# Decay products and one key-value product over 128 tokens in a fused recurrence and two-layer network kernel, with a third PSUM bank for the first matmul of a step

## The chip, the cores and the metric

The kernel runs on one core of a Trainium2 chip. The metric is device time in microseconds (us) of one execution, as the median of several. The engines go by their names in the profile: PE (matmul), PEld (its weight load), DVE (vector), ACT (activation), POOL (GpSimd) and SP, which here only issues DMAs.

## The reference

Inputs are double precision for the weights and single precision for the rest. Three parts follow one another:

```
state = 0                                   # per batch (4) and head (8), 48 x 48
for t in range(768):
    y[t]  = r[t] @ (state + (u * k[t]) (x) v[t])
    state = w[t][:, None] * state + k[t] (x) v[t]
x = y as 3072 x 384
h = x @ w_in;  g = h if h >= 1, 0 if h <= -1, else (h + 1)^2 / 4;  x = g @ w_out     # 384 -> 2048 -> 384
h = x @ w2_in; g = h * sigmoid(1.702 h);                            out = g @ w2_out
```

w lies between 0.8 and 0.95, so the product of the decays over 128 tokens gets very small (0.8 to the power 128 is 4e-13).

## The kernel before, in words

**The recurrence** (`window(n)`, lines 406 to 538) is done in 24 windows of 128 tokens (6 per batch), each for all 8 heads. A window has two chunks of 64 tokens, c = 0 and c = 1. Heads are paired: `hh` says which half of the partitions a head has, `m` which of the four pairs. The decays are multiplied up inside each chunk: a scan from the right (line 423) gives `rr`, the product of the decays to the end of the chunk, its reciprocal seeds a scan from the left (425) that gives `pp`. k is multiplied by `rr` (430, DVE, in place) and r by `pp`: in place for windows 0 to 6 (433, one 128x512 on POOL), into the tiles `ra` for the later ones (437, two 64x512 on POOL). `pcs` is a copy of the eight chunk products (429, DVE). PE then transposes k (464, tile `tp`, copied to `ktok` by ACT, 471) and forms the scores (469, tile `sc`); DVE's masked copy puts the scores into the other half of `ra` (474), over a diagonal that POOL writes there (455). For windows 0 to 6 ACT copies the scaled r into `ra` after the scores (484). PE multiplies keys by values for both chunks (498, one PSUM tile per chunk, rows 64c to 64c+63 of the array, the four pairings of row half and column half in the order of `ORDER`), and y for chunk 0 (504). The operand `lt` of the y product holds, per chunk, the state (48 partitions of one half) and the values (64 partitions of the other half). The state goes on by `upd(c)` (510, DVE: `lt` of chunk c plus the key-value product into the tile `us`) and `put(us, c)` (446, POOL: `us` times `pcs` into `lt` of a chunk): `put(carry, 0)` at the start of a window, `put(upd(0), 1)` in the middle. ACT sums squares of the decays (449, 450) and of r and k (486) for a check of the number range.

**The two layers** go by `step(s)` (260): a step is one tile of 384 tokens and one of 16 slices of 128 hidden columns; 8 tiles make 128 steps per layer. Step s issues, in this order: `gemm1` into the PSUM tile `hp` (651, nine matmuls of 384 columns: each operand is split in a high and a low part), DVE's clamp (688) and ACT's square (689) of it, the low part of g of the step before (676, on POOL and DVE by turns), then one turn of the recurrence, `gemm2` of step s-3 into the three accumulators (660, nine matmuls; 669 in the second layer), DVE's maximum with `hp` (701), which is the last reader of `hp`, ACT's high part of g (682), weight work and, in every second step, one more turn of the recurrence. `hp` comes from a pool of two PSUM banks by turns, so `gemm1` of a step waits for line 701 of two steps before. In a turn every running window goes on to its next `yield`; a new window starts when the one before has had eight turns (four at the very start). The recurrence for tile i+1 runs beside the first layer of tile i.

**The weights** come as double precision and are put together as single precision: DVE 638, ACT 640, DVE 642, POOL 644 (`wide`). The first layer's 32 pieces are done in the opening, the second layer's (`conv_w2`, 194) one in every second step of tiles 1 to 6: the four operations, ACT's check of the piece (147, 148), the load of a new piece and the store to `w2_d` (196) are issued in the same step.

**PSUM** has eight banks: three accumulators, two for `hp`, three (`ps_s`) for `tp`, `sc`, `yt`, `kv0` and `kv1`. When the recurrence is over, `hp` has four.

**Order.** Up to step 15 a planner orders the instructions of each engine by modelled times and priorities (the opening). From step 16 on (`manual_schedule`) each engine does its instructions in the order of the program.

Of the kernel before, what the change touches and what calls it, by code (L numbers as in the profile page):

```python
# [9 lines left out]
F32 = mybir.dt.float32  # L10
# [3 lines left out]
AF = mybir.ActivationFunctionType  # L14
# [16 lines left out]
WW = MC * (C + 1)  # L31
# [3 lines left out]
ORDER = ((0, 0), (0, 1), (1, 1), (1, 0))  # L35
PMIN = 1e-10
# [14 lines left out]
K_E = (1,)  # L51
PI_B = 1
RIP_N = 7
# [48 lines left out]
def fast_path(st, tc, rkw_t, nat, v_l, w1, w2, u, out, x2_d, w2_d, flag_i, force):  # L102
# [4 lines left out]
    ps_h = st.enter_context(tc.tile_pool(name="ps_h", bufs=2, space=PSUM))  # L107

# [41 lines left out]
    def to_f32(l, n):  # L150
# [9 lines left out]
        wide(nc, [x[1:] for x in todo])  # L160
# [4 lines left out]
        return [(x[0], x[3].bitcast(F32)) for x in todo]  # L165
# [27 lines left out]

    def conv_w2():
        for i, wf in to_f32(1, PRE_N):
            nc.sync.dma_start(out=w2_d[:, i, :], in_=wf)

# [24 lines left out]
    pools = {"h": [ps_h], "x2": None}  # L222
# [37 lines left out]
    def step(s):  # L260
# [79 lines left out]
    with ExitStack() as sa:  # L340
        at = sa.enter_context(tc.tile_pool(name="at", bufs=1))
        a2 = sa.enter_context(tc.tile_pool(name="a2", bufs=2))
        ps_s = sa.enter_context(tc.tile_pool(name="ps_s", bufs=3, space=PSUM))
# [9 lines left out]
        lt = [at.tile([128, 2, MC * D + 16], F32, name=f"lt{i}") for i in range(2)]  # L353

        def slots(t, a, j):
            return t[:, a:a + WW].rearrange("p (a b) -> p a b", b=C + 1)[:, :, j]

        def consts():
# [9 lines left out]
            nc.vector.memset(slots(one_s, 1, C), 1.0)  # L368
# [23 lines left out]
        def load_v(n):  # L392
# [4 lines left out]
            for hh in range(2):  # L397
                p = slice(64 * (1 - hh), 64 * (1 - hh) + 64)
                nc.sync.dma_start(out=lt[i][p, hh, 0:MC * D], in_=v_l[n, hh])
# [6 lines left out]
        def window(n):  # L406
# [10 lines left out]
            pi = a2.tile([128, 2 * WW + 1], F32, tag="pi", name="pi", bufs=PI_B)  # L417
            pp, rr = pi[:, 0:WW], pi[:, WW:]
            pcs = a2.tile([128, MC], F32, tag="pcs", name="pcs")
# [9 lines left out]
            nc.vector.tensor_copy(pcs, slots(rr, 1, 0))  # L429
            eng_of(K_E, n).tensor_tensor(out=kt, in0=kt, in1=rr[:, 1:].rearrange("p (a b) -> p a b", b=C + 1)[:, :, 1:C + 1], op=ALU.mult)  # L430
            pr = pp.rearrange("p (a b) -> p a b", b=C + 1)[:, :, 0:C]
# [432 lines left out]
```

## Time and profile before

| | us |
|---|---|
| median of 3 runs (1035.96 to 1038.11) | 1036.93 |
| the profiled execution | 1035.07 |
| its span, first to last instruction | 1033.3 |
| PE busy in the span | 950.6 (92%) |
| DVE busy | 604.1 (58%) |
| ACT busy | 517.5 (50%) |
| POOL busy | 469.6 (45%) |

The span is the time between the first and the last instruction; 1.8 us of the profiled execution lie outside it. Matmuls overlap, so PE's busy time is read together with its waits. Several engines wait for each other at any time; only what PE or the engine that limits a stage waits for can lengthen the span.

### The profile page before, as it was taken

How to read it: one execution, taken by the hardware profiler on the slowest of the kernel's cores; microseconds unless marked ns; L12 is line 12 of the kernel's file. 1: busy time of each engine (PE TensorE's matmuls, PEld its weight loads, DVE VectorE, ACT ScalarE, POOL GpSimd, SP SyncE). 2: the span in 40 equal slices, each digit the busy share in tenths (PEclk: the TensorE clock that was granted, in tenths of full speed). 3: DMA queues.
4: the chain of work that ended last, by engine and by line, in shares of the span. 5: the costliest groups of instructions: out<-in, count | busy, mean ns of one | idle time of the engine just before them, and what ended most of it. 6: DMA issues, size and time to landing. Idle time of an engine off the chain costs nothing.

```text
span 1033.3 us, 18712 instructions
## 1 busy us (share of the span) xinstructions
PE 950.6 (92%) x6976; PEld 903.7 (87%) x6976; DVE 604.1 (58%) x1007; ACT 517.5 (50%) x1221; POOL 469.6 (45%) x481
## 2 busy tenths in 40 slices
PE   4645889999999999999999999999999999999997
PEld 2434769989888988898989999999999999999997
DVE  8999984787877777778674663323232323232321
ACT  5654554565555655546653565455555433333332
POOL 6897872676676666766662342111111111111111
PEclk8756989999999999999999999999999999999999
DMA  9763422644534545434310543232323110101000
GB/s 250 203 191 107 129 56 56 188 126 128 145 103 110 147 129 142 131 103 126 101 43 5 167 153 108 62 107 62 108 62 109 30 46 1 47 2 46 15 9 27
DMA packets 52228, 100.20 MB, mean 97 GB/s; under 512 B 8608, under 2 KB 34464, under 8 KB 52128
## 3 DMA queue, kind: packets, MB, share of 16 engines
q1 hardware_dynamic: 52128, 98.91, 33.2%
q8 instruction: 57, 0.93, 0.4%
q14 instruction: 43, 0.35, 0.1%
HBM read 81.97 MB, written 15.73 MB: 95 GB/s over the span
## 4 chain that ended last, share of the span: by engine, by line
PE 57%; DVE 17%; POOL 8%; ACT 6%; issue 6%; DMA 4%; SPq 2%; POOLq 0%; ACTq 0%; DVEq 0%
PE hp L651 27%; PE acc L669 20%; PE acc L660 8%; DVE pi L423 2%; DVE t L701 2%; ACT gh L682 2%; DVE ra L474 2%; DVE pi L425 2%; DVE gl L676 1%; DVE wt L638 1%; DMA wst<-w 1%; POOL ra L437 1%; POOL rkn L426 1%; POOL wt L644 1%; DVE wt L642 1%
## 5 line engine op out<-in xcount | busy, mean ns | idle before, releaser
L676 POOL TENSOR_TENSOR gl<-t,gh 128x384 fp32r<-128x384 f32 x128 | 132.0, 1031 | 387.7 <-ACT gh L682 386.1
L682 ACT ACTIVATE gh<-t 128x384 fp32r<-128x384 f32 x256 | 133.9, 523 | 205.5 <-DVE t L701 122.9
L712 DVE TENSOR_TENSOR t<-t,hp 128x384 f32<-128x384 f32 x128 | 70.8, 553 | 218.6 <-ACT t L707 218.1
L707 ACT ACTIVATE t<-hp 128x384 f32<-128x384 f32 x128 | 63.0, 492 | 145.8 <-PE hp L651 145.8
L660 PE MATMUL acc<-gh,whi 128*128 128x384 f32 x384 | 132.4, 350 | 0.3 <-DVE ev L252 0.3
L660 PE MATMUL acc<-gl,whi 128*128 128x384 f32 x384 | 130.2, 339 | 1.2 <-DVE gl L676 1.2
L669 PE MATMUL acc<-wlo,gh 128*128 128x384 f32 x384 | 130.2, 339 | 0.0
L669 PE MATMUL acc<-whi,gh 128*128 128x384 f32 x384 | 129.9, 338 | 0.0
L660 PE MATMUL acc<-gh,wlo 128*128 128x384 f32 x384 | 129.6, 338 | 0.0
L669 PE MATMUL acc<-whi,gl 128*128 128x384 f32 x384 | 129.3, 337 | 0.0
L651 PE MATMUL hp<-xh,whi 128*128 128x384 f32 x384 | 95.9, 359 | 24.1 <-DVE t L701 23.0
L676 DVE TENSOR_TENSOR gl<-t,gh 128x384 fp32r<-128x384 f32 x128 | 81.4, 636 | 47.0 <-ACT gh L682 44.6
L689 ACT ACTIVATE t<-t 128x384 f32<-128x384 f32 x128 | 66.3, 518 | 78.7 <-DVE t L688 76.8
L701 DVE TENSOR_TENSOR t<-t,hp 128x384 f32<-128x384 f32 x128 | 70.1, 548 | 51.9 <-ACT t L689 51.1
L644 POOL TENSOR_TENSOR wt<-wt,wb 128x384 int32<-128x384 int32 x64 | 71.7, 1121 | 62.0 <-ACT wb L640 51.1
L651 PEld LDWEIGHTS hp<-xh,whi 128*128 128x128 f32 x384 | 67.8, 193 | 33.3 <-DVE t L701 29.9
L688 DVE TENSOR_SCALAR t<-hp 128x384 f32<-128x384 f32 x128 | 70.4, 550 | 41.7 <-PE hp L651 41.6
L651 PE MATMUL hp<-xl,whi 128*128 128x384 f32 x384 | 90.2, 344 | 0.0
L651 PE MATMUL hp<-xh,wlo 128*128 128x384 f32 x384 | 89.4, 341 | 0.0
L651 PE MATMUL hp<-x2l,whi 128*128 128x384 f32 x384 | 88.8, 339 | 0.0
L651 PE MATMUL hp<-x2h,wlo 128*128 128x384 f32 x384 | 88.0, 337 | 0.0
L651 PE MATMUL hp<-x2h,whi 128*128 128x384 f32 x384 | 87.4, 335 | 0.0
(106 smaller groups left out, 1944.3 us busy)
## 6 DMA issues: line engine op xcount, KB each, us to landing
wst<-w SPq DMA_DIRECT2D x96, 384.0 KB, 3.4
rk<-rkw_t SPq DMA_DIRECT2D x48, 289.7 KB, 4.9
rkn<-nat SPq DMA_DIRECT2D x24, 384.0 KB, 4.1
w_d<-wt SPq DMA_DIRECT2D x32, 192.0 KB, 3.3
w2f<-w_d SPq DMA_DIRECT2D x32, 192.0 KB, 2.5
vn<-nat SPq DMA_DIRECT2D x24, 192.0 KB, 3.0
lt<-v_l SPq DMA_DIRECT2D x48, 96.0 KB, 3.0
x_d<-ev SPq DMA_DIRECT2D x24, 192.0 KB, 2.5
```

Source lines behind the costliest of these rows:

```text
L423: nc.vector.tensor_tensor_scan(out=rr[:, WW:0:-1], data0=ws[:, WW:0:-1], data1=one_s[:, WW:0:-1], initial=0.0, op0=ALU.mult, op1=ALU.max)
L644: nc.gpsimd.tensor_tensor(out=t, in0=t, in1=b, op=ALU.add)
L651: nc.tensor.matmul(out=hp[:, 0:n], lhsT=win(a, f, kk), rhs=b[:, kk, 0:n], start=(i == 0), stop=(i == 3 * KD - 1))
L660: nc.tensor.matmul(out=acc[j][:, 0:n], lhsT=wout(a, f, j * 128, 128), rhs=b[:, 0:n], start=(f == 0 and i == 0), stop=(f == KF - 1 and i == 2))
L669: nc.tensor.matmul(out=o[:, 0:DM], lhsT=a[:, j * 128:(j + 1) * 128], rhs=wout(b, f, 0, DM), start=(f == 0 and i == 0), stop=(f == KF - 1 a ...
L676: eng.tensor_tensor(out=gl[:, 0:n], in0=t[:, 0:n], in1=gh[:, 0:n].bitcast(F32), op=ALU.subtract)
L682: nc.scalar.activation(out=gh[:, 0:n], in_=t[:, 0:n], func=AF.Copy)
L688: nc.vector.tensor_scalar(t[:, 0:n], hp[:, 0:n], scalar1=-1.0, scalar2=1.0, op0=ALU.max, op1=ALU.min)
L689: nc.scalar.activation(out=t[:, 0:n], in_=t[:, 0:n], func=AF.Square, bias=0.5, scale=0.5)
L701: nc.vector.tensor_tensor(out=t[:, 0:n], in0=t[:, 0:n], in1=hp[:, 0:n], op=ALU.max)
L707: nc.scalar.activation(out=t[:, 0:n], in_=hp[:, 0:n], func=AF.Sigmoid, scale=1.702)
L712: nc.vector.tensor_tensor(out=t[:, 0:n], in0=t[:, 0:n], in1=hp[:, 0:n], op=ALU.mult)
```

## The change

The decays are multiplied up over the whole window of 128 tokens. r is scaled in place in all windows, by one POOL instruction, and copied to `ra` by ACT two turns later and ahead of the scores. Chunk 1's operand `lt` is then `lt` of chunk 0 plus the key-value product of chunk 0, written by DVE's `upd(0)` itself, without a `put`. The state after the window takes one key-value product over all 128 tokens (all 128 rows of the array) in place of the one over the second 64. `pcs` has four elements and is copied by ACT. The two key-value products share one PSUM tile, issued chunk 0 first; `ps_s` has two banks, and the third goes to `hp`. `lt` has 64 columns per chunk instead of 48, in the load too. POOL's addition for a weight piece is issued a step after the other operations, and its store a step after that.

```diff
-WW = MC * (C + 1)
+WW = NP * (W + 1)
-PMIN = 1e-10
+PMIN = 1e-15
+DSC = 1e-5
-K_E = (1,)
-RIP_N = 7
+    ps_c = st.enter_context(tc.tile_pool(name="ps_c", bufs=1, space=PSUM))
...
+    adds, puts = [], []
     def conv_w2():
-        for i, wf in to_f32(1, PRE_N):
+        adds.extend(to_f32(1, PRE_N, adds_later=True))
+    def add_w2():
+        while puts:
+            i, wf = puts.pop(0)
             nc.sync.dma_start(out=w2_d[:, i, :], in_=wf)
+        while adds:
+            i, t, b = adds.pop(0)
+            nc.gpsimd.tensor_tensor(out=t, in0=t, in1=b, op=ALU.add)
+            puts.append((i, t.bitcast(F32)))
-    pools = {"h": [ps_h], "x2": None}
+    pools = {"h": [ps_h, ps_h, ps_c], "x2": None}
...
+                add_w2()
                 if f in PRE_F and nconv[1] < NPC:
                     conv_w2()
...
-        ps_s = sa.enter_context(tc.tile_pool(name="ps_s", bufs=3, space=PSUM))
+        ps_s = sa.enter_context(tc.tile_pool(name="ps_s", bufs=2, space=PSUM))
-        lt = [at.tile([128, 2, MC * D + 16], F32, name=f"lt{i}") for i in range(2)]
+        lt = [at.tile([128, 2, MC, 64], F32, name=f"lt{i}") for i in range(2)]
...
-            nc.vector.tensor_copy(pcs, slots(rr, 1, 0))
-            eng_of(K_E, n).tensor_tensor(out=kt, in0=kt, in1=rr[:, 1:].rearrange("p (a b) -> p a b", b=C + 1)[:, :, 1:C + 1], op=ALU.mult)
-            if n < RIP_N:
-                nc.gpsimd.tensor_tensor(out=rt, in0=rt, in1=pr, op=ALU.mult)
-            else:
-                for hh in range(2):
-                    p = slice(64 * hh, 64 * hh + 64)
-                    nc.gpsimd.tensor_tensor(out=ra[hh][p], in0=rt[p], in1=pr[p], op=ALU.mult)
+            nc.scalar.activation(out=pcs, in_=slots(rr, 1, 0), func=AF.Copy)
+            nc.vector.tensor_tensor(out=kw, in0=kw, in1=rr[:, 1:].rearrange("p (a b) -> p a b", b=W + 1)[:, :, 1:W + 1], op=ALU.mult)
+            nc.gpsimd.tensor_tensor(out=rw, in0=rw, in1=pp.rearrange("p (a b) -> p a b", b=W + 1)[:, :, 0:W], op=ALU.mult)
...
-            nc.scalar.activation(out=pp, in_=pp, func=AF.Square, accum_out=stat[:, n, 0:1])
-            nc.scalar.activation(out=rr[:, 1:], in_=rr[:, 1:], func=AF.Square, accum_out=stat[:, n, 3:4])
+            nc.scalar.activation(out=sq, in_=sq, func=AF.Square, scale=DSC, accum_out=stat[:, n, 0:1])
...
+            if first:
+                for hh in range(2):
+                    nc.gpsimd.memset(lt[i][64 * hh:64 * hh + 64, hh], 0.0)
             if PUT == 0 and not first:
-                put(carry.pop(), 0)
+                put(carry.pop())
+            for hh in range(2):
+                p = slice(64 * hh, 64 * hh + 64)
+                nc.scalar.activation(out=ra[hh][p], in_=rt[p], func=AF.Copy)
...
-            if first:
-                for hh in range(2):
-                    nc.gpsimd.memset(lt[i][64 * hh:64 * hh + 64, hh], 0.0)
...
-            if n < RIP_N:
-                for hh in range(2):
-                    p = slice(64 * hh, 64 * hh + 64)
-                    nc.scalar.activation(out=ra[hh][p], in_=rt[p], func=AF.Copy)
-            sq = rk[i][:, 0:OW]
-            nc.scalar.activation(out=sq, in_=sq, func=AF.Square, accum_out=stat[:, n, 1:2])
+            nc.scalar.activation(out=rw, in_=rw, func=AF.Square, scale=DSC, accum_out=stat[:, n, 1:2])
+            nc.scalar.activation(out=kw, in_=kw, func=AF.Square, accum_out=stat[:, n, 3:4])
...
-            yt = ps_s.tile([128, NP, W], F32, tag="s", name="yt")
-            kv = [ps_s.tile([128, NP, D], F32, tag="s", name=f"kv{c}") for c in range(1 if last else NC2)]
+            kvt = ps_s.tile([128, NC2, NP, D], F32, tag="s", name="kv")
+            kv = [kvt[:, c] for c in range(1 if last else NC2)]
             def mm_kv():
-                for m in range(NP):
-                    for c, hh in (ORDER if len(kv) == 2 else ORDER[:2]):
-                        nc.tensor.matmul(out=kv[c][64 * hh:64 * hh + D, m, :], lhsT=kn_t[64 * c:64 * c + 64, m, 64 * hh:64 * hh + D], rhs=vn[64 * c:64 * c + 64, m, hh, :], start=True, stop=True)
+                for c in range(len(kv)):
+                    q = slice(0, 64 * (c + 1))
+                    for m in range(NP):
+                        for hh in range(2):
+                            nc.tensor.matmul(out=kv[c][64 * hh:64 * hh + D, m, :], lhsT=kn_t[q, m, 64 * hh:64 * hh + D], rhs=vn[q, m, hh, :], start=True, stop=True)
...
-                    nc.vector.tensor_tensor(out=us[p], in0=lt_s(lt[i], hh, c), in1=kv[c][p], op=ALU.add)
+                    nc.vector.tensor_tensor(out=us[p] if c else lt_s(hh, 1), in0=lt_s(hh, 0), in1=kv[c][p], op=ALU.add)
...
             mm_kv()
+            yt = ps_s.tile([128, NP, W], F32, tag="s", name="yt")
+            upd(0)
             mm_y(0)
-            put(upd(0), 1)
...
-    pools["h"].append(st.enter_context(tc.tile_pool(name="ps_h2", bufs=2, space=PSUM)))
+    pools["h"].append(st.enter_context(tc.tile_pool(name="ps_h2", bufs=1, space=PSUM)))
```

## Rows read from the trace of the kernel before

**Rows 1.** Busy time of each engine in three stretches (windows view): us, busy (xinstructions), clock, DMA.

```profile
0.00:151.00 151.00, 92.10 (x815) 72.05 (x815) 140.82 (x197) 79.33 (x177) 118.65 (x121) 0.76 0.58 158
...
200.00:553.00 353.00, 337.72 (x3083) 314.52 (x3082) 265.37 (x460) 203.21 (x513) 235.80 (x246) 1.00 0.42 116
553.00:1033.00 480.00, 472.89 (x2688) 472.21 (x2686) 166.47 (x294) 211.79 (x480) 93.80 (x92) 1.00 0.20 63
```

**Rows 2.** Waits in 200 to 553 us: who waited for whom, us, times, longest.

```profile
POOL wt L644 <- ACT wb L640: 45.2, 23, 2.8
...
PEld hp L651 <- DVE t L701: 14.8, 17, 1.5
...
PEld yt L504 <- POOL lt L446: 4.1, 7, 0.9
...
PEld yt L504 <- POOL lt L477: 2.8, 4, 0.9
...
PEld kv L498 <- ACT ktok L471: 0.7, 3, 0.3
```

**Rows 3.** PE in order of time, 475 to 499 us: start, us, instruction, count, wait.

```profile
475.34 0.57 PE L498 MATMUL kv<-vn,ktok 64*48 64x48 f32 x32
475.85 0.69 PE L504 MATMUL yt<-ra,lt 128*64 128x64 f32 x16
476.46 0.44 PE L660 MATMUL acc<-gh,whi 128*128 128x384 f32 x1
...
485.10 0.34 PE L660 MATMUL acc<-gh,wlo 128*128 128x384 f32 x1
486.44 0.80 PE L651 MATMUL hp<-xh,whi 128*128 128x384 f32 x3 [0.99 <-DVE t L701]
...
497.60 0.33 PE L504 MATMUL yt<-ra,lt 128*64 128x64 f32 x2 [0.74 <-POOL lt L446]
```

**Rows 4.** POOL in order of time, 491 to 498 us.

```profile
491.78 1.00 POOL L644 TENSOR_TENSOR wt<-wt,wb 128x384 int32<-128x384 int32 x1 [2.37 <-ACT wb L640]
...
496.93 1.20 POOL L446 TENSOR_TENSOR lt<-us,pcs 48x192 f32<-48x192 f32 x2
```

**Rows 5.** PE in a batch's last window, where only chunk 0 has a key-value product.

```profile
408.82 0.56 PE L498 MATMUL kv<-vn,ktok 64*48 64x48 f32 x16
409.31 0.69 PE L504 MATMUL yt<-ra,lt 128*64 128x64 f32 x16
```

**Rows 6.** A group of instructions, whole span: count, busy us, mean ns, idle before.

```profile
L484 ACT ACTIVATE ra<-rk 64x512 f32<-64x512 f32 x14 | 8.7, 623 | 0.8 <-POOL rk L433 0.7
```

**Rows 7.** ACT in order of time: the copy that the key-value product of Rows 3 needs.

```profile
474.29 0.58 ACT L471 ACTIVATE ktok<-tp 128x512 f32<-128x512 f32 x1
```

**Rows 8.** Groups in the opening (0 to 165 us), DVE and POOL.

```profile
L642 DVE SCALAR_TENSOR_TENSOR wt<-wst,wt 128x384 int32<-128x384 int32 x32 | 30.2, 947 | 0.4
L638 DVE TENSOR_SCALAR wt<-wst 128x384 int32<-128x384 int32 x32 | 24.4, 773 | 0.3 <-DMA wst<-w 0.2
...
L429 DVE COPY pcs<-pi 128x8 f32<-128x8 f32 x8 | 5.1, 632 | 0.1
...
L446 POOL TENSOR_TENSOR lt<-us,pcs 48x192 f32<-48x192 f32 x22 | 19.0, 863 | 4.0 <-PE yt L504 3.0 <-DVE us L510 0.2
```

**Rows 9.** Two of the same groups in 200 to 553 us.

```profile
L642 DVE SCALAR_TENSOR_TENSOR wt<-wst,wt 128x384 int32<-128x384 int32 x30 | 20.7, 690 | 1.0
L638 DVE TENSOR_SCALAR wt<-wst 128x384 int32<-128x384 int32 x30 | 12.0, 401 | 0.0
```

**Rows 10.** Two windows meeting in the opening (PE, ACT, DVE in order of time).

```profile
87.03 1.33 PE L469 MATMUL sc<-rk 48*64 48x64 f32 x20
91.36 0.33 PE L504 MATMUL yt<-ra,lt 128*64 128x64 f32 x2
...
101.43 0.58 ACT L522 ACTIVATE xr<-yt 128x512 f32<-128x512 f32 x1
...
103.36 1.48 DVE L474 COPY_PREDICATED ra<-mask,sc 64x512 f32<-64x512 int32 x2
```

More of the change, by code (lines that the diff above doesn't have):

```diff
@@ L148, in check_w, with to_f32 @@
         nc.scalar.activation(out=jk, in_=jk, func=func, scale=-1.0, accum_out=wmin[:, c:c + 1])
-    def to_f32(l, n):
+    def to_f32(l, n, adds_later=False):
         todo = []
@@ L159, in to_f32 @@
             todo.append((i, raw[:, :, 1].bitcast(I32), raw[:, :, 0], t, b))
-        wide(nc, [x[1:] for x in todo])
+        wide(nc, [x[1:] for x in todo], not adds_later)
         for i, top, low, t, b in todo:
@@ L164, in to_f32 @@
             load_w(l)
-        return [(x[0], x[3].bitcast(F32)) for x in todo]
+        return [(x[0], x[3], x[4]) if adds_later else (x[0], x[3].bitcast(F32)) for x in todo]
     def split_w(i, wf):
@@ L367, in consts @@
             nc.vector.memset(one_s, PMIN)
-            nc.vector.memset(slots(one_s, 1, C), 1.0)
+            nc.vector.memset(slots(one_s, 1, W), 1.0)
             nc.vector.memset(seed, PMIN)
@@ L398, in load_v @@
                 p = slice(64 * (1 - hh), 64 * (1 - hh) + 64)
-                nc.sync.dma_start(out=lt[i][p, hh, 0:MC * D], in_=v_l[n, hh])
+                nc.sync.dma_start(out=lt[i][p, hh], in_=v_l[n, hh])
         tile_of = {}
@@ L468, in window @@
                     p = slice(64 * hh, 64 * hh + D)
-                    nc.tensor.matmul(out=sc[64 * (1 - hh):64 * (1 - hh) + 64, mc, :], lhsT=kt[p, mc, :], rhs=(rt[p, mc, :] if n < RIP_N else ra[hh][p, mc, :]), start=True, stop=True)
+                    nc.tensor.matmul(out=sc[64 * (1 - hh):64 * (1 - hh) + 64, mc, :], lhsT=kt[p, mc, :], rhs=rt[p, mc, :], start=True, stop=True)
             kn_t = a2.tile([128, NP, 128], F32, tag="ktok", name="ktok", bufs=1)
@@ L503, in mm_y @@
                         mc = m * NC2 + c
[L504 removed]
+                        nc.tensor.matmul(out=yt[64 * hh:64 * hh + 64, m, c * C:(c + 1) * C], lhsT=lt[i][:, hh, mc, :], rhs=ra[hh][:, mc, :], start=True, stop=True)
             def upd(c):
[L507 removed]
+                us = a2.tile([128, NP, D], F32, tag="us", name="us") if c else None
                 for hh in range(2):
                     p = slice(64 * hh, 64 * hh + D)
[L510 removed]
+                    nc.vector.tensor_tensor(out=us[p] if c else lt_s(hh, 1), in0=lt_s(hh, 0), in1=kv[c][p], op=ALU.add)
                 return us
             mm_kv()
+            yt = ps_s.tile([128, NP, W], F32, tag="s", name="yt")
+            upd(0)
             mm_y(0)
[L515 removed]
             yield
@@ L633, in fast_path, with wide @@
                 nc.vector.tensor_copy(flag_i, okf)
-def wide(nc, todo):
+def wide(nc, todo, add=True):
     for top, low, t, b in todo:
@@ L642, in wide @@
         nc.vector.scalar_tensor_tensor(out=t, in0=top, scalar=-0x40000000, in1=t, op0=ALU.bitwise_and, op1=ALU.bitwise_or)
-    for top, low, t, b in todo:
+    for top, low, t, b in todo if add else ():
         nc.gpsimd.tensor_tensor(out=t, in0=t, in1=b, op=ALU.add)
```

38 lines of the change are left out of this document (19 added, 19 removed).

## The prediction

> **What bounds the kernel now.** I read the busy time by stage first [rows 1]. From 553 us on PE is busy nearly throughout (472.9 of 480 us), so nothing that the change does there can shorten the span. From 200 to 553 us PE is the busiest engine too (337.7 of 353), but with gaps, and the recurrence runs beside the first layer. Up to 151 us (the opening) DVE is the bound: 140.8 us busy of 151, while PE has 92.1 and a clock of 0.76 of full speed.
>
> Then the waits of the middle stage, for those of PE alone [rows 2]. PEld waits 14.8 us in 17 places for line 701 before it can start a step's `gemm1`, because the bank of `hp` is still being read, and 6.9 us (4.1 + 2.8) for POOL's writes of `lt` before a y product. The large waits of the other engines (POOL 45.2 us for ACT in the weight addition) matter only through what stands behind them.
>
> Last, PE in order of time. A wait for `hp` looks like this [rows 3]: a matmul starts at 485.10 and the next only at 486.44, 0.99 us of it being put down to line 701. The wait for `lt` is there too: y starts at 497.60 after 0.74 us that are put down to POOL's `put`. Its cause is ahead of it on POOL [rows 4]: the weight addition has idled POOL for 2.37 us, waiting for ACT, with the rest of the window's POOL work behind it, so that `put` comes only at 496.93.
>
> **The change part by part.** The sum is made against the profiled execution, 1035.07 us (a span of 1033.3 and 1.8 around it), which lies 1.9 us under the median of 1036.93.
>
> *Third bank of `hp`, the middle stage.* `gemm1` of step s now waits for line 701 of step s-3, a whole step (over 3 us) more slack, against waits of at most 1.5 us [rows 2]. What is late next is `gemm2` of step s-3, which needs the low part of g, and that was issued a step earlier than it is used. Of the 14.8 us I let 1.0 stay: -13.8. Bounds: 0 (the lag shows up at another operand) and -14.8.
>
> *`lt`.* `upd(0)` writes chunk 1's operand itself; POOL loses two of four `put` instructions per window and, from window 7 on, half of the r product; the memset of a first window comes two turns earlier; the weight addition no longer waits in POOL's queue, as its inputs are a step old, and the store behind it on SP finds its data ready, so that SP's loads of v and its moves of `xr` aren't held up by it. All three causes of the 6.9 us go; I leave 0.9 for places where POOL's low part of g stands ahead of `put`: -6.0. Bounds 0 and -6.9.
>
> *The key-value product.* This is PE time on the path, and it grows. Today the four pairings of row half and column half follow each other: 16 products, 32 records, are through in 0.51 us (475.34 to 475.85) [rows 3]. In a batch's last window only chunk 0 is done, 8 products in the same row half with alternating columns, exactly the new form of chunk 0: they take 0.49 us (408.82 to 409.31) [rows 5], as long as twice as many. The new chunk 1 takes all 128 rows. No row shows that with 48 columns; with 64 columns y does, 0.61 us for 8 products (475.85 to 476.46) [rows 3]. Bounds: 0.25 (half of today's 0.51) and 0.61. I take 0.49, as its column halves alternate like those of rows 5. So a product costs 0.98 instead of 0.51, +0.47 (0.23 to 0.59), in all but the last window of a batch. After 151 us there are 15 of these: +7.1 us, bounds +3.5 to +8.9. The Trainium skill, "TensorEngine Tiling (Array Packing)", section "Instruction Overhead", says that a matmul of one column takes as long as one of 60; by that the 48 columns of chunk 1 would be charged as 60 of y's 64, an estimate of 0.57 us, and the sum would be 1.2 us higher. No row here shows which.
>
> *ACT.* From window 7 on it takes two copies of `ra` (0.62 us each [rows 6]; the earlier windows have them now) and in all windows `pcs`: four elements per partition, between 0 and 0.62, say 0.3. The squares are regrouped from three instructions into three of the same total width: nothing. That is 1.5 us for each of some 16 windows in the middle stage, 24 us on an engine that is busy 203 of 353 [rows 1]. The idle time hides it, with one exception: `ktok`. It ends at 474.87 [rows 7], 0.47 ahead of the product that needs it, and already costs PE 0.7 us in three windows [rows 2]. Bounds: 0, and 16 times (1.5 - 0.47), 17 us. I take +1.5, because the new copies stand a turn ahead of the scores, and ACT no longer waits in that place for two POOL instructions but for one. The other wait that is added, `pcs` on ACT for DVE's first scan, has only work behind it that needs DVE's later instructions anyway.
>
> *Two banks for the window.* `tp` now needs `kv` of the window before read by `upd(1)`, `sc` needs its `yt` copied out. In the middle stage a window's scores come five turns after the window before has done that: nothing. DVE loses `pcs` there, but DVE isn't the bound.
>
> *Sum of the middle stage:* -13.8 - 6.0 + 7.1 + 1.5 = -11.2 us.
>
> *The opening.* DVE loses eight copies `pcs` of 0.63 us: -5.1 [rows 8]. POOL loses the `put` of chunk 1, 12 of the 22 instructions at 0.86 us, 10.4 of its 118.7 us. DVE's weight operations are slow while POOL is busy: 947 and 773 ns against 690 and 401 in the middle stage [rows 8, 9], 32 of each, 20.1 us in all, with POOL busy 79% of the time against 67% [rows 1]. With 10.4 us less POOL would be at 72%, which on a straight line gives back 0.58 of the 20.1, 11.8 us; the other bound is 0, since fewer but equally placed POOL instructions can meet the same operations. I take -3, nearer to 0, as those operations and POOL's additions belong to the same pieces. The planner orders everything anew, with two banks where three are used today: bounds 0 and +26 (below), I take +2. Opening: -6.1 (-17 to +18). The wider load of v, more than a third up from 96 KB, lies in a DMA share of 0.58 [rows 1]: nothing.
>
> *Total:* -17.3: 1017.8 in a profiled execution, 1019.6 as a median.
>
> **The rivals.**
> 1. *The opening shrinks with POOL's work.* DVE and POOL hold each other up, and DVE's operations speed up in proportion: -5.1 - 11.8 in the opening. For it: `pcs`, eight elements per partition, takes 0.63 us on average there [rows 8]. Against it: the pieces' own POOL additions stay. 1036.9 - 11.2 - 16.9 = 1008.8. The Trainium skill, "SBUF — State Buffer", section "Who interferes with whom", says that a port pair is shared by the two engines as an exclusive lock and that the loser "fully blocks" until the instruction ends; by that rule each POOL instruction less is a block less. The trace agrees in kind (773 ns against 401), no row shows the proportion.
> 2. *The waits move.* DVE and ACT lag by bursts, and PE, a step further ahead, waits the same time for the low part of g, `ktok` or the scores. For it: `ktok` has 0.47 us to spare [rows 7]. Against it: DVE is busy 265 of 353 us [rows 1], and its lag is 1.5 us at most where PE feels it [rows 2]. -17.3 + 13.8: 1033.4.
> 3. *The other side: two banks make the opening serial.* Today the scores of a window start at 87.03, ahead of y of the window before at 91.36 [rows 10]; with two banks they must wait for that y and for ACT's copy of it at 101.43. At 4.3 us for each of the six windows that the opening can hold that is +26, and -11.2 - 8.1 + 26 gives +6.7: 1043.6. It decides from 3.2 us per window on. For it: the chain runs through each window. Against it: the scores' reader on DVE starts at 103.36 today, ten microseconds after the scores [rows 10], so DVE's queue, not the bank, sets the pace; and y no longer waits for a `put`.
> 4. *The third bank isn't used in turn.* The list has the two-bank pool twice and the new one once, indexed by the step modulo 3, so each bank comes up every third step; this I give no more than the rest.
>
> **How the numbers follow.** Forecast 0.55, rival 1 0.13, rival 2 0.15, rival 3 0.11, the rest 0.06. The predicted time is the forecast's, 1019.6. The range reaches down to rival 1 with the key-value product at its lower bound (1008.8 - 3.6, 1005) and up to rival 2 (1034); rival 3 and the tails lie outside. A measurement here can tell some 0.2% (2 us) from no change. Forecast and rival 1 are faster, rival 2 mostly; half of rival 3 and of the rest is slower, and where rival 3 is half true the gains cancel it: faster 0.84, same 0.07, slower 0.09.
>
> **What would show it.** PEld's waits for line 701 in the middle stage under 2 us; those for `lt` under 1; the key-value product at 0.9 to 1.1 us for 32 records; the time between the first scans of successive batches, two tiles apart, down by some 4 us; POOL's weight addition without a wait for ACT; `pcs` gone from DVE, and DVE's end of the opening some 6 us earlier; the stretch of the second layer as long as before. Wrong I would be if PE's waits in the middle stage add up to 20 us again under other names, or if the opening ends later than 151 us, with DVE idle in it.

## The result, and the profile after

The changed kernel takes 1027.17 us (median of four runs, 1026.75 to 1028.37); the kernel before, on the same chip, 1036.45 (four runs, one more than in the table above). The ratio is 0.9909, with a 95% interval of 0.9895 to 0.9923. It is faster, in the predicted direction and inside the range, but 7.6 us short of the predicted 1019.6. The profiled execution, the longest of the four, has a span of 1026.7 us, 6.6 less than that of before.

The windows view of the changed kernel, the same first two stretches as [rows 1] and the rest of the span (us, busy time of PE, PEld, DVE, ACT and POOL, granted clock, DMA share, GB/s):

```profile
0.00:151.00 151.00, 94.95 (x828) 75.57 (x829) 137.79 (x195) 82.73 (x189) 108.82 (x111) 0.79 0.61 164
200.00:553.00 353.00, 343.06 (x3058) 324.95 (x3057) 256.57 (x446) 220.75 (x552) 187.06 (x198) 0.99 0.42 117
553.00:1027.00 474.00, 466.92 (x2654) 466.24 (x2652) 163.84 (x289) 209.37 (x476) 91.80 (x90) 1.00 0.20 63
```

Beside [rows 1], POOL has lost work in both first stretches, ACT has gained some, and PE is *busier* in the middle although it should have had less to wait for. A stretch of fixed times mixes different work once the opening is shorter, so from here on the kernels are compared between two events that they all have: ACT's first copy of `acc` for the first tile (the opening ends there) and for the seventh (the middle stage ends). First the kernel before, then the changed one, between those events:

```profile
181.99:573.77 391.78, 376.00 (x3349) 351.48 (x3348) 290.31 (x506) 219.31 (x549) 251.15 (x261) 1.00 0.42 117
```

```profile
176.88:567.80 390.92, 380.98 (x3349) 361.90 (x3348) 279.16 (x490) 240.01 (x599) 199.28 (x211) 0.99 0.42 120
```

So the opening is 5.1 us shorter (predicted 6.1), the middle stage only 0.9 (predicted 11.2), and what follows it is 459 us in both (459.6 and 458.9). In the middle stage PE's time without work fell by 5.8 us (15.78 to 9.94), and its busy time rose by 5.0. The waits of that stage in the changed kernel (who waited for whom, total us, times, longest):

```profile
PEld kv L505 <- issue: 6.3, 7, 1.8
PE kv L505 <- DVE ra L486: 4.4, 5, 1.5
PE yt L511 <- DVE ra L486: 4.0, 4, 1.7
PEld yt L511 <- POOL lt L452: 3.5, 2, 1.8
...
PEld kv L505 <- ACT ktok L483: 2.0, 4, 0.9
```

The waits for `hp` of [rows 2] are gone entirely. PE now waits for `ra`, which DVE completes with the scores (y needs it, and so does a key-value product that gets the PSUM bank of the scores), and in two places for `lt`, once for 1.8 us, longer than any wait of before. And the granted clock has come off 1.00. Three stretches of six microseconds (us, PE busy, clock), and one of the waits ahead of them in PE's order of time:

```profile
204.00:210.00 6.00, 5.86 (x64) 0.72 0.54 147
358.00:364.00 6.00, 5.38 (x34) 0.72 0.34 102
491.00:497.00 6.00, 5.00 (x32) 0.72 0.12 31
```

```profile
492.00 0.83 PE L511 MATMUL yt<-ra,lt 128*64 128x64 f32 x16 [1.74 <-DVE ra L486]
...
493.25 0.52 PE L668 MATMUL acc<-gl,whi 128*128 128x384 f32 x1
```

Within each stretch the clock fell from 2.4 to 1.2 GHz for a while, behind waits of 1.49, 1.57 and 1.74 us; a matmul that starts every 0.175 us elsewhere then starts every 0.32. At a mean of 0.72 each stretch loses (1 - 0.72) x 6 = 1.7 us of PE's work, 5.0 in all. The kernel before has no such stretch in its middle stage.

The key-value product, PE in order of time:

```profile
181.00 1.06 PE L505 MATMUL kv<-vn,ktok 64*48 64x48 f32 x32
181.88 0.65 PE L511 MATMUL yt<-ra,lt 128*64 128x64 f32 x16
```

It takes 0.88 us, against 0.51 [rows 3] and the forecast 0.98. Fourteen such products lie in the middle stage: 5.2 us. Together with the 5.0 of the clock that is twice the rise of PE's busy time; what fell by as much was not worked out.

**Where the wait for `ra` comes from.** POOL and then DVE of the changed kernel, in order of time, around 355 us:

```profile
345.88 1.47 POOL L204 TENSOR_TENSOR wt<-wt,wb 128x384 int32<-128x384 int32 x1
352.04 1.01 POOL L545 TENSOR_TENSOR xl<-xr,xh 128x384 fp32r<-128x384 f32 x1 [4.69 <-ACT xh L544]
353.12 1.38 POOL L461 TENSOR_SCALAR_AFFINE_SELECT ra<-bb 64x512 f32<-64x512 f32 x2
354.47 1.01 POOL L684 TENSOR_TENSOR gl<-t,gh 128x384 fp32r<-128x384 f32 x1
355.43 1.01 POOL L204 TENSOR_TENSOR wt<-wt,wb 128x384 int32<-128x384 int32 x1
356.40 1.40 POOL L452 TENSOR_TENSOR lt<-us,pcs 48x192 f32<-48x192 f32 x2
```

```profile
354.91 1.95 DVE L684 TENSOR_TENSOR gl<-t,gh 128x384 fp32r<-128x384 f32 x1 [0.18 <-ACT gh L690]
356.89 1.48 DVE L486 COPY_PREDICATED ra<-mask,sc 64x512 f32<-64x512 int32 x2
```

POOL idles for 4.69 us, then has five pieces of work in a row, with the weight addition (L204), now a step late, between the low part of g and `put`. DVE's own low part of g takes 1.95 us beside them, where most others of the same shape in this stage take 0.56, and the scores' copy into `ra` stands behind it. In this place y waited for that copy, which ends at 358.37; `put` had ended at 357.80. The Trainium skill, "SBUF — State Buffer", section "Who interferes with whom", says that a DVE instruction with two SBUF inputs contends with a POOL instruction that reads SBUF; the pair at 354.91 agrees in kind, with its factor of 3.5.

### The profile page after: what moved, and what is told of

The parts are those of the page before. It is cut to its first block, busy times and chain, and to the rows that moved or that the text cites. A ratio compares the mean times of both kernels' runs of the same rounds, so it can differ in the third digit from the quotient of the medians.

```text
span 1026.7 us, 18669 instructions
## 1 busy us (share of the span) xinstructions
PE 953.9 (93%) x6976; PEld 913.5 (89%) x6976; DVE 587.1 (57%) x983; ACT 540.0 (53%) x1279; POOL 404.0 (39%) x416
## 4 chain that ended last, share of the span: by engine, by line
PE 62%; DVE 15%; ACT 8%; DMA 5%; issue 5%; SPq 3%; POOL 1%; ACTq 0%; DVEq 0%; POOLq 0%
PE hp L659 29%; PE acc L677 20%; PE acc L668 10%; DMA rk<-rkw_t 3%; SPq L533 3%; DVE pi L433 2%; DMA xr<-xr 2%; DVE ra L486 2%; DVE wt L646 2%; DVE t L709 2%; ACT gh L690 2%; ACT ra L469 1%; DVE pi L435 1%; ACT t L697 1%; PE yt L511 1%
## 5 line engine op out<-in xcount | busy, mean ns | idle before, releaser
L684 POOL TENSOR_TENSOR gl<-t,gh 128x384 fp32r<-128x384 f32 x128 | 134.5, 1051 | 438.4 <-ACT gh L690 427.8
L668 PE MATMUL acc<-gl,whi 128*128 128x384 f32 x384 | 132.6, 345 | 1.3 <-DVE gl L684 1.1
L668 PE MATMUL acc<-gh,wlo 128*128 128x384 f32 x384 | 131.9, 343 | 0.0
L684 DVE TENSOR_TENSOR gl<-t,gh 128x384 fp32r<-128x384 f32 x128 | 78.4, 612 | 57.2 <-ACT gh L690 55.9
L659 PE MATMUL hp<-xh,whi 128*128 128x384 f32 x384 | 93.5, 353 | 11.3 <-DVE t L709 11.3
L659 PEld LDWEIGHTS hp<-xh,whi 128*128 128x128 f32 x384 | 69.9, 195 | 13.6 <-DVE t L709 12.1
L668 PEld LDWEIGHTS acc<-gh,whi 128*128 128x128 f32 x384 | 73.0, 191 | 5.4 <-ACT ev L263 1.4
```

What stands on the lines that cost most here:

```text
L659: nc.tensor.matmul(out=hp[:, 0:n], lhsT=win(a, f, kk), rhs=b[:, kk, 0:n], start=(i == 0), stop=(i == 3 * KD - 1))
L668: nc.tensor.matmul(out=acc[j][:, 0:n], lhsT=wout(a, f, j * 128, 128), rhs=b[:, 0:n], start=(f == 0 and i == 0), stop=(f == KF - 1 and i == 2))
L684: eng.tensor_tensor(out=gl[:, 0:n], in0=t[:, 0:n], in1=gh[:, 0:n].bitcast(F32), op=ALU.subtract)
```

## Experiments

All twelve were timed against the kernel before, which had medians of 1036.22 (e1 to e4), 1037.33 (e5 to e9) and 1036.31 us (e10 to e13). "Opening" is the time of ACT's first copy of the first tile's `acc`, "middle" the time from there to that of the seventh, both in the profiled execution; "clock" is the PE work lost there at the lower clock, summed from stretches of 1 us as above. What follows the middle is 459 us in every kernel (458.8 to 459.6). The profiled execution is not the median one: it lies 1.2 us above the median for the changed kernel, 3.4 for e2 (the longest of twelve) and 4.0 for e11, and 2.3 and 1.8 below for e13 and e12. So the stages of one execution each say little about differences of a microsecond or two.

| kernel | median us | ratio, 95% interval | opening | middle | clock |
|---|---|---|---|---|---|
| before | 1036.45 | | 182.0 | 391.8 | 0 |
| changed | 1027.17 | 0.9909 [0.9895, 0.9923] | 176.9 | 390.9 | 5.1 |
| e1_banks | 1027.99 | 0.9914 [0.9898, 0.9929] | 175.7 | 392.1 | 5.1 |
| e2_copies_late | 1035.99 | 0.9989 [0.9976, 1.0002] | 172.1 | 406.8 | 9.9 |
| e3_two_hp | 1030.25 | 0.9936 [0.9920, 0.9952] | 177.8 | 390.9 | 0 |
| e4_adds_same | 1022.18 | 0.9862 [0.9842, 0.9882] | 175.6 | 385.0 | 0 |
| e5_adds_behind | 1026.65 | 0.9894 [0.9879, 0.9910] | 175.3 | 391.5 | 5.1 |
| e6_two_hp_adds_same | 1023.86 | 0.9867 [0.9853, 0.9882] | 177.9 | 385.4 | 0 |
| e7_kv_quarters | 1019.41 | 0.9825 [0.9812, 0.9837] | 174.7 | 383.9 | 0 |
| e9_check_late | 1042.09 | 1.0048 [1.0032, 1.0065] | 174.5 | 407.5 | 13.4 |
| e10_quarters_full | 1030.45 | 0.9934 [0.9917, 0.9952] | 185.8 | 384.5 | 0 |
| e11_store_late | 1021.79 | 0.9854 [0.9836, 0.9873] | 176.7 | 388.2 | 3.4 |
| e12_pcs_dve | 1019.24 | 0.9836 [0.9817, 0.9855] | 171.9 | 384.9 | 0 |
| e13_r_products | 1026.34 | 0.9903 [0.9884, 0.9922] | 174.7 | 388.2 | 3.4 |

The theory that the first four runs start from (A, where an expectation uses a letter) is that what the change brings in takes the gain back: two banks shared by a window's four tiles, and the weight addition's new place. Each expectation names the rival that it is set against.

### e1_banks: fixed banks for the window's tiles

```
-ps_s bufs=2, tag "s" for tp, sc, kv, yt
+ps_s bufs=1, tag "s0" for tp and kv, "s1" for sc and yt
```

> The changed kernel, but the window's two PSUM banks are given by hand: one for tp and kv, one for sc and yt. In the changed kernel the planner put kv into the bank of the scores in every third window (n = 8, 11, 14, 17, 20), and there PE waits 0.7 to 1.5 us for DVE's copy of the scores before the key-value product. Theory A (the expected gain was given back by waits of the new two-bank rotation, by late scores, and by the clock that drops behind long waits): these five waits go, the middle stage (evacuation of tile 0 to that of tile 6, 390.9 us in the changed kernel) shortens by 4 to 7 us, the total is 1020 to 1023. Theory B (DVE and ACT lag by bursts and PE waits the same time at whatever operand comes next): y of the same windows waits instead, the middle stage stays within 1 us.

1027.99 us, as the changed kernel. The waits at the key-value product turned into waits for the keys and for `ra`: PE waits 6.3 us for `ra` in y, and PEld 6.3 for `ktok` and 5.5 for `lt`. Which bank `kv` gets sets the name of a wait, not its length. The bank part of the theory falls.

### e2_copies_late: ACT's copies of r behind the scores

```
-            [turn ahead of the scores] nc.scalar.activation(out=ra[hh][p], in_=rt[p], func=AF.Copy)
+            [turn behind the scores]   nc.scalar.activation(out=ra[hh][p], in_=rt[p], func=AF.Copy)
```

> The changed kernel, but ACT's copies of the scaled r into ra are issued after the scores, ahead of the squares, where the kernel before had them for its first windows. Theory A (the early copies stand on ACT ahead of the square of a step and so delay DVE and the scores' copy in windows 15 and 21, where y waits 1.6 to 1.8 us and the clock drops): those two waits and their slow stretches go, 4 to 7 us less, 1020 to 1023. Theory B (ACT is late in these windows anyway): the copies now stand between the scores and y, y waits in more windows, and the time is 0 to 6 us longer, 1027 to 1033.

1035.99 us, longer than either theory had: 8.8 slower than the changed kernel, and by the middle stage of the profiled execution, the longest of twelve, 15.9 (the opening, ordered anew, is 4.8 shorter). Once the copies are made by ACT at all, they have to be early; issued behind the scores they take back nearly all that the change gained.

### e3_two_hp and e4_adds_same: the two causes apart

e3 takes the third bank of `hp` back and gives the window three; e4 leaves the banks and puts the weight addition and its store back into the step of their conversion:

```
-        adds.extend(to_f32(1, PRE_N, adds_later=True))
+        for i, wf in to_f32(1, PRE_N):
+            nc.sync.dma_start(out=w2_d[:, i, :], in_=wf)
```

> The changed kernel, but hp has two banks again and the window three. Theory A (the third bank takes away the 14.8 us of waits for hp in the middle stage; what came back is the window's own): the waits for line 709 before gemm1 come back with 12 to 15 us, the waits of kv for the scores' copy go, total 1031 to 1038. Theory B (waits only move): other waits of PE shrink by as much as the hp waits grow, total 1024 to 1029.

> The changed kernel, but a weight piece's addition on POOL and its store are issued in the same step as the other operations again. POOL then waits for ACT again (some 40 us in the middle stage). Theory A (POOL's queue was what made put late): PE's waits for lt and for the scores' copy grow, 2 to 6 us more, 1029 to 1033. Rival: with half the r product and half the puts gone from POOL the wait has slack and nothing changes, within 1 us of 1027.

In e3 PEld's waits for `hp` are back, 13.1 us in 17 places, and the middle stage takes the same 390.9 us as with the third bank; the 1030.25 us lie between the ranges of its two theories. In e4 the stage takes 385.0, the clock stays at 1.00, and the kernel beats both others with 1022.18, which neither side of its expectation had. POOL and DVE of e4, in order of time, in the place shown above for the changed kernel:

```profile
347.67 1.00 POOL L653 TENSOR_TENSOR wt<-wt,wb 128x384 int32<-128x384 int32 x1 [2.48 <-ACT wb L649]
349.28 1.02 POOL L546 TENSOR_TENSOR xl<-xr,xh 128x384 fp32r<-128x384 f32 x1 [0.60 <-ACT xh L545]
350.37 1.38 POOL L462 TENSOR_SCALAR_AFFINE_SELECT ra<-bb 64x512 f32<-64x512 f32 x2
351.72 1.00 POOL L685 TENSOR_TENSOR gl<-t,gh 128x384 fp32r<-128x384 f32 x1
352.69 1.39 POOL L453 TENSOR_TENSOR lt<-us,pcs 48x192 f32<-48x192 f32 x2
```

```profile
352.15 0.99 DVE L685 TENSOR_TENSOR gl<-t,gh 128x384 fp32r<-128x384 f32 x1 [0.18 <-ACT gh L691]
353.17 1.48 DVE L487 COPY_PREDICATED ra<-mask,sc 64x512 f32<-64x512 int32 x2
```

In its own step the addition fills the gap in which POOL waits for ACT's `xh` anyway. The wait for `wb` that I had wanted to remove (2.48 us here) cost nothing: the next instruction on POOL could not have started before 349.2, when ACT's `xh` ended. Of the stage's 32 additions in e4, five stand ahead of such a gap; the others have POOL's next instruction right behind them. Over the whole stage POOL's waits for `wb` went from 50.3 us in the kernel before to none in the changed one, and those for `xh` and `gh` from 51.2 to 127.7. A step later the addition leaves that gap empty and lands ahead of `put`. Whether it costs by its place in POOL's queue or by what it does to DVE's low part of g beside it (1.95 us, 0.99 in e4) was not tried apart. The instructions on PE, DVE and ACT stand in the same order in e4 and in the changed kernel; only POOL's and SP's differ.

### e5, e11: place and lateness of the addition, and the store

e5 keeps the addition one step late (a second list holds the fresh pieces) and issues it at the end of a step, where a second turn has been issued if the step has one; e11 puts only the addition back and leaves the store late:

```
e5:  -                add_w2()    [ahead of the conversion]
     +                add_w2()    [at the end of the step]
     ...
e11: -        adds.extend(to_f32(1, PRE_N, adds_later=True))
     +        adds.extend(to_f32(1, PRE_N))    [addition at once]
     +        puts.extend(adds)                [in add_w2: store a step later]
```

> The changed kernel with one thing moved: the weight addition and the store behind it are still a step late, but they are issued at the end of a step, behind the second turn of the recurrence, instead of ahead of the first. Theory (the place costs, not the lateness: ahead of the turn the addition comes in the same stretch as POOL's low part of g and its put of lt, and y waits behind them): about as fast as with the addition in its own step, 1021 to 1024 us, no stretch at a granted clock of 0.50, PE's wait for lt under 2 us in the middle stage. Rival (any late place costs the same, as the planner or POOL's queue meets it elsewhere): 1026 to 1028, with one or more stretches at 0.50. If the clock stretches go and the time stays, the waits have moved.

> The changed kernel with the weight addition back in the step of its conversion, and only the store on SP a step late. Theory (it is POOL's order that costs: the late addition leaves POOL idle while it waits for xh and then stands between the low part of g and put): as e4, 1021 to 1024, the addition again in POOL's gap ahead of xl, no stretch at a granted clock of 0.50. Rival (the store's place on SP, with the loads behind it, was what counted): as the changed kernel, 1026 to 1028.

e5 gave 1026.65 us and the three slow stretches again, but it told nothing about the place: the pieces are converted in odd steps, which have a second turn, and added in even ones, which have none, so that POOL's order in the middle stage is exactly that of the changed kernel. e11 gave 1021.79, like e4, with e4's order on POOL: it is the addition, not the store. Its expectation of no slow clock failed, and that shows what the clock costs. The same instructions, first in e11, then in e4, PE in order of time:

```profile
223.72 1.06 PE L503 MATMUL kv<-vn,ktok 64*48 64x48 f32 x32 [0.52 <-ACT ktok L481]
225.56 0.78 PE L509 MATMUL yt<-ra,lt 128*64 128x64 f32 x16 [0.79 <-DVE ra L484]
...
226.68 0.52 PE L666 MATMUL acc<-gl,whi 128*128 128x384 f32 x1
```

```profile
222.73 1.06 PE L506 MATMUL kv<-vn,ktok 64*48 64x48 f32 x32 [0.51 <-ACT ktok L484]
224.58 0.78 PE L512 MATMUL yt<-ra,lt 128*64 128x64 f32 x16 [0.79 <-DVE ra L487]
...
225.56 0.34 PE L669 MATMUL acc<-gl,whi 128*128 128x384 f32 x1
```

The waits are equal to 0.01 us, and in one execution the clock fell, in the other it didn't. The profiled execution of e11 was the longest of its five, 1025.74 us; the other four lie between 1020.83 and 1021.96. It lost 3.4 us to the clock and its middle stage is 3.2 us longer than e4's: what PE lost to the clock in this stage reached the end here. (e11's second fall came behind waits of 1.22 and 0.77 us.)

### e6: the price of the third bank without the late addition

e4 with the banks of e3 (`hp` on two, the window on three).

> The kernel with the addition in its own step (e4), and the banks as before the change: hp on two, the window on three. Neither of the two should have a stretch at a granted clock of 0.50, so their difference is the price of the third bank alone. Theory 1 (waits are conserved in part: without the bank PE waits for hp 12 to 15 us, but then less for ktok, r and lt): 1024 to 1027, 2 to 5 us above e4. Theory 2 (the third bank gives what its waits say): 1033 to 1036, 11 to 14 above e4. Rival (it gives nothing): 1021 to 1023.

1023.86 us, between two of its ranges and 1.7 above e4; middle 385.4 against e4's 385.0. PE's waits changed names, first e6, then e4:

```profile
PEld hp L659 <- DVE t L709: 9.5, 15, 1.0
PE hp L659 <- DVE t L709: 4.5, 14, 0.7
...
PEld kv L505 <- ACT ktok L483: 1.3, 2, 1.1
```

```profile
PEld kv L506 <- ACT ktok L484: 6.7, 10, 1.1
...
PE kv L506 <- ACT ktok L484: 3.6, 6, 0.8
PE yt L512 <- DVE ra L487: 3.1, 5, 0.8
...
PEld yt L512 <- POOL lt L453: 2.6, 3, 0.9
```

Together with e3 that makes a square: middle 390.9 and 390.9 with the addition late (three banks, two banks), 385.0 and 385.4 with it in its step. The addition is worth 5.5 to 5.9 us, the third bank 0.0 to 0.4. With three banks the granted clock accounts for 5.1 of the 5.9 (PE's busy time is 3.6 us longer than in e4, its time without work 2.3); with two the clock holds, and PE is without work for 11.5 us in e3 and 5.9 in e6, 4.1 of the difference in waits for `hp`. The medians agree on the addition, 5.0 and 6.4 us (5.4 with e11, in whose profiled execution the stage took 388.2), though some of them are from different sets, whose kernels before differ by up to 1.1 us. They are kinder to the bank, 3.1 and 1.7, though 0.9 and 2.3 us of that lie in the openings of the profiled executions, which the planner had ordered differently. A bank worth 13.8 us is out either way.

### e7, e10: the key-value product in quarters

e6 with two `kv` tiles and the order of before, 64 rows to a product. e7 leaves out the first chunk's product from the state carried on; e10 computes everything:

```
e7, e10:  -                    q = slice(0, 64 * (c + 1))
          +                            q = slice(64 * c, 64 * c + 64)
          ...
e10:      -                    nc.vector.tensor_tensor(out=us[p] if c else lt_s(hh, 1), in0=lt_s(hh, 0), in1=kv[c][p], op=ALU.add)
          +                    nc.vector.tensor_tensor(out=us[p] if c else lt_s(hh, 1), in0=lt_s(hh, c), in1=kv[c][p], op=ALU.add)
```

> e6 with the key-value product in the order of before: two tiles, 64 rows per product, the four pairings of row half and column half following each other. LEAVES OUT the first chunk's product from the state that a window hands on, so the output differs. The product should take 0.51 us for its 32 records instead of 0.88. Theory (the product is PE time on the path): 15 products of 0.37 us less, 1017.5 to 1021.5 if e6 gives 1025, 4 to 6 us less than e6. Rival (PE then waits that much longer for r or lt in y): within 1 us of e6.

> The quarters of e7 with the whole computation: the state carried on adds the second half's product to the operand that already holds the first (one operand of DVE's addition is another slice, no instruction more). Additions and stores in their own step, hp on two banks, the window on three. Theory: as e7, 1018 to 1021, the product at 0.51 us; faster than the kernel before, the changed kernel and e4 (1022.2). Rival (DVE's second addition, now behind its first, delays the state and so y): 1022 to 1025, with PE's wait for lt above e7's 2.9 us.

PE's busy time in the middle stage falls by 5.6 us, as it should (e6, then e10):

```profile
177.89:563.24 385.35, 379.42 (x3349) 356.16 (x3348) 274.23 (x490) 240.31 (x598) 205.54 (x211) 1.00 0.45 122
```

```profile
185.75:570.27 384.52, 373.77 (x3349) 351.35 (x3348) 274.74 (x490) 240.04 (x599) 210.59 (x211) 1.00 0.44 121
```

The stage itself gets only 0.8 us shorter (1.4 in e7): PE then waits 3.8 us for `ra` and 2.9 for `lt` in both. The rival of e7 holds in this stage, although the 1019.41 us lie in the theory's range. The 4.5 us by which e7 beats e6 came mostly from the opening (3.2), and e10's loss of 11 against e7 is the opening too, 185.8 against 174.7: the planner had ordered that part anew, and in e10 badly (DVE waits 12.1 us for PE there, 5.6 in e7). e10's expectation failed for a reason that has nothing to do with the product.

### e9: ACT's checks of a weight piece a step later

e4, with the checks and the load behind them in the steps that convert nothing.

```
             if l == 1:
+                checks.append((i, top))
+                continue
...
+            if l == 0 and i >= 1 and f not in PRE_F:
+                while checks:
+                    check_w(1, *checks.pop(0))
+                    load_w(1)
```

> e4, and in the middle stage ACT's two checks of a weight piece (1.9 us) with the load that follows them are issued a step after the piece's conversion, in the steps that convert nothing. Theory (ACT's burst of conversion, checks, xh and copies of r is what keeps PE waiting for ktok, r and the squares of g): 4 to 7 us less than e4, 1015 to 1018, the wait for ktok under 2 us. Rival (ACT's burst is hidden and the waits move): within 1 us of e4. Possible harm: the next piece's load comes a step later and DVE's conversion waits for its DMA, 2 us or more above e4.

1042.09 us, the slowest of all. Neither side of the expectation holds, and the harm that it feared, DVE waiting for a piece's DMA, is not among the waits of that stage. The checks moved out of one burst and into another, ahead of the keys' copy:

```profile
PEld kv L513 <- ACT ktok L491: 18.9, 10, 3.6
PE kv L513 <- DVE ra L494: 8.2, 4, 3.3
PE kv L513 <- ACT ktok L491: 7.7, 6, 2.4
```

ACT's queue has no room to spare just ahead of the keys' copy, 1.3 us in front of it at 360.15 us being enough. That ACT's burst is what sets the 385 us is not shown by this run, and which chain of the other engines does was not settled.

### e12, e13: `pcs` back on DVE, r's products back on POOL

Both on e4. e12 undoes `pcs` on ACT; e13, from the eighth window on, lets POOL write r's product into the operand of y, as before, without copies on ACT (the square of the scaled r is then taken of the unscaled r):

```
e12: -            nc.scalar.activation(out=pcs, in_=slots(rr, 1, 0), func=AF.Copy)
     +            nc.vector.tensor_copy(pcs, slots(rr, 1, 0))
e13: +                    nc.gpsimd.tensor_tensor(out=ra[hh][p], in0=rw[p], in1=pr[p], op=ALU.mult)
     -                nc.scalar.activation(out=ra[hh][p], in_=rt[p], func=AF.Copy)
```

> e4 with the small copies pcs back on DVE. The prediction's step (eight copies at 0.63 us on the engine that bounds the opening): the first evacuation 4 to 6 us later than e4's 175.6 us, nothing in the middle stage, 1026 to 1028 in all. Rival (DVE's copies lie in its own gaps, and the opening gained by POOL's fewer instructions): within 1.5 us of e4 in the opening and in all.

> e4 with r treated as in the kernel before from the eighth window on: POOL writes its product with the decay into the operand of y in two instructions, the scores read that, and ACT makes no copies there. The square of the scaled r is taken of r without its decay. The prediction's step (copies on ACT cost 1.5 us at most, POOL's relief is worth more): 1023 to 1028, PE's waits for lt and r above e4's 5.7 us. Rival (ACT's burst is what PE waits for, so 1.25 us a window less on ACT is worth more than POOL's two instructions cost): 1015 to 1020, the wait for ktok under 3 us instead of 10.

e12 should have given the opening its 5 us back; in the profiled execution, the shortest of its five, it is 3.7 us *shorter*, and at 1019.24 us it is the fastest kernel of the study that computes everything. The eight copies took 212 ns each this time (DVE, opening):

```profile
L440 DVE COPY pcs<-pi 128x4 f32<-128x4 f32 x8 | 1.7, 212 | 0.0
```

Both its theory and its rival fall, but they were not tried alone: the planner ordered the opening anew. e13 gave 1026.34 us, 4.2 more than e4, with the waits for `lt` up (PEld 3.7, PE 2.9) and the one for `ktok` almost as long (6.3): the prediction's side. Moving r's work from POOL to ACT gains 3.2 us in the middle stage of the profiled executions, where e13 lost 3.4 to the clock and e4 none. As e11 shows, that loss can differ between executions, so the sign rests on the medians.

## Why the prediction was right, and where it was not

The direction was right, and the time lies in the range because the range reached up to rival 2. The forecast's own mechanism did not hold: of its -11.2 us the middle stage gave -0.9, and 1027.17 lies about halfway between the forecast (1019.6) and rival 2 (1033.4).

**Third bank of `hp` (-13.8, bounds 0 and -14.8).** The waits went, as forecast, and the time did not: 0.0 to 0.4 us in this stage, 3.1 at most by a whole kernel's median. This is the step that failed most. It took the length of the waits for their price. Rival 2's mechanism (the waits move, to `ktok`, the scores and `ra`) is what the runs show, and the argument against it, that DVE lags by 1.5 us at most, only says how long a single wait was. The bound at 0 was right.

**`lt` (-6.0).** Three causes stood in one number. The third, "the weight addition no longer waits in POOL's queue", has the wrong sign: moved a step, it costs 5.5 to 5.9 us. The 45.2 us of waits for ACT in [rows 2] were no price: with the addition back in its place, and POOL waiting again, the kernel is faster (e4). In the place shown it had filled a gap that POOL has anyway; for the other places that is argued from the waits that came up under other names. r's product in place gains about 3 (e13, the clock included). The two `put` instructions less were not tried alone. If the measured terms are added (0.4 for the bank, 0.8 for the product, 5.9 for the addition, 3.2 for r), 4 us of gain are left for them and the rest of that group. That group and r together can be read from e10, which has neither the third bank nor the late addition nor the wider product, but the rest of the change: its middle stage is 7.3 us shorter than that of the kernel before (384.5 against 391.8, no clock lost in either). So the rest of the change gave more than the -6.0 and +1.5 forecast for it, and the late addition took most of it back.

**Key-value product (+7.1, bounds 3.5 and 8.9).** 0.88 us instead of 0.98: the first chunk took the predicted 0.49, the second 0.39 (e6, PE in order of time, the second chunk and what follows):

```profile
509.89 0.56 PE L505 MATMUL kv<-vn,ktok 128*48 128x48 f32 x16
510.28 0.65 PE L511 MATMUL yt<-ra,lt 128*64 128x64 f32 x16
```

The 48 columns of 128 rows are cheaper than the 64 of y by more than their number (0.39 to 0.61). The prediction's estimate of 0.57, from what the Trainium skill, "TensorEngine Tiling (Array Packing)", section "Instruction Overhead", says of 60 columns, does not hold here; the measurement decides. Whether that statement or its scaling from y's time is at fault, no run shows. But 5.2 us of work is not 5.2 us of time: undone, it gave 0.8 to 1.4 of the stage. The step's "PE time on the path" was wrong there: PE would have waited for `ra` and `lt` instead.

**ACT (+1.5).** The sign of this part is better than I thought (e13), under the condition that I gave, that the copies stand a turn ahead of the scores; e2 prices that condition at 15.9 us of the middle stage in its longest execution, and at 8.8 by the medians of the whole kernel.

**The two banks for the window (0 in the middle, +2 in the opening).** Right as far as the openings tell: kernels with three take 174.7 to 185.8 us there (e3, e6, e7, e10), kernels with two 171.9 to 176.9. Rival 3 is out. (It priced a window at the 4.3 us to y, although it has the scores wait for ACT's copy too, 14.4 us after them.)

**Opening (-6.1).** The size came out, -5.1, the reasons did not; that is luck. Contention (-3) gave nothing: the two weight operations of [rows 8] took 30.2 + 24.4 us before and take 25.9 + 28.5 now, while the two scans, which had no term, went from 29.3 to 23.7. DVE's operations of the opening after:

```profile
L646 DVE TENSOR_SCALAR wt<-wst 128x384 int32<-128x384 int32 x32 | 28.5, 900 | 4.4 <-DMA wst<-w 2.9 <-POOL wlo L177 1.4
L650 DVE SCALAR_TENSOR_TENSOR wt<-wst,wt 128x384 int32<-128x384 int32 x32 | 25.9, 820 | 0.3
L433 DVE TENSOR_TENSOR_SCAN pi<-rk,one_s 128x516 f32<-128x516 f32 x8 | 13.4, 1676 | 0.6 <-DMA rk<-rkw_t 0.6
...
L435 DVE TENSOR_TENSOR_SCAN pi<-rk,seed 128x516 f32<-128x516 f32 x8 | 10.3, 1292 | 0.0
```

And for `pcs` (-5.1) nothing speaks: back on DVE in e12 the eight copies took 1.7 us, and the opening was not longer; in an opening of the same order they were not tried. Five kernels whose work stands in the same order there (the changed one, e4, e5, e9, e11) have openings of 174.5 to 176.9 us in one execution each; kernels that the planner orders differently have anything from 171.9 to 185.8. The opening is set by that order more than by any term of my sum. Which waits in it decide was not isolated. (The bounds written for the opening, -17 to +18, leave out that contention could give nothing: by the terms' own bounds the upper end is +20.9.)

**The clock** was no term at all, and 5.1 us of PE's work were lost to it (e3, without that loss, takes as long). Several points named beforehand failed: PEld's wait for `lt` stayed above 1 us (3.5), the product came out just under its 0.9, and the first scans of the third and fourth batch lie 132.5 us apart against 133.2, not 4 less. The sign of being wrong, 20 us of PE's waits under other names, was not clear enough to decide: from 200 to 553 us the listed waits of PE add up to 9.2 us (15.2 before), those of PEld to 23.1 (33.6 before). POOL's addition does go without a wait for ACT, and what follows the middle stage is as long as before, as forecast.

## What to carry to other kernels

A wait on the busiest engine is not worth its length until taking it away has been tried; where several engines run close together, the same few microseconds stand in the list under whichever name comes last. An instruction that waits at the head of a queue that keeps its order may be sitting in a gap that would be empty without it, so look at what the queue does next before it is moved "out of the way". And when a planner orders the work anew, compare event to event in the stage that was edited, or its 14 us from build to build in another stage will be taken for the effect of the edit.

## What was unexpected of the hardware

TensorE's clock fell to 1.2 GHz within a stage in which PE is busy 97% of the time, each time behind a wait or two around the key-value product and y (1.49, 1.57 and 1.74 us in the changed kernel; 0.52 and 0.79 with the product between them ahead of one of e11's two falls), at 1.7 us of work lost each time. The same two waits in e4 left it at 2.4 GHz, so here a wait's length alone did not decide.
